# S4D convolution and PEER expert layer on one core: indices spread through DRAM, expert products on partitions, output as three rounded products

## The chip, the cores and the metric

The kernel runs on one core of a Trainium2 chip. The metric is the device time of one execution in microseconds. The core has five engines that run side by side, each in its own order: TensorE (PE in the rows, PEld for its weight loads), VectorE (DVE), ScalarE (ACT), GpSimd (POOL) and SyncE (SP), which here issues nearly all transfers.

## The reference

Sequence length 2048, width 512. Two stages with residuals; cut to what matters:

```
h  = x + S4D(layernorm(x))            # long convolution: kernel from 128 complex modes per channel, FFT of length 4096
xf = layernorm(h)
q  = einsum("nd,dhc->nhc", xf, w_q)   # 32 heads, two halves of 128
s1 = q[..., :128] . k1^T ; s2 = q[..., 128:] . k2^T     # 16 scores each
e  = 16*argmax(s1) + argmax(s2)       # one expert of 256 per token and head
act = gelu(einsum("nd,nhd->nh", xf, u[e]))
out = h + einsum("nh,nhd->nd", act, v[e])               # softmax over one candidate is 1
```

Since only one expert is chosen per head, the kernel needs per token only how often each of the 256 experts was chosen: `out = h + sum_e count[n,e] * gelu(xf[n]·u[e]) * v[e]`.

## The kernel before

**First part (to about 313 us).** The convolution as a two-step transform by matmuls, with tables of modes that POOL, ACT and DVE make (`factors`, `tables`, `kgen`, `u_s1` ... `k_ia`), and `w_piece`, which folds the keys into `w_q` and stores the product in DRAM (`w_d`).

**Second part (313 us to the end): the expert layer.** Eight blocks b of 256 tokens. Names end in the block's number, those of score work in 2b+k for its two halves of 128 tokens. For one block, in order of data:

- `prefetch`: `Tb`, `cb`, `xt` are loaded. `inverse`: 64 small matmuls (`ib`), DVE adds `xt`: `h`.
- `center`: POOL sums the four pieces of `h` (`hs`), a matmul with ones gives `mean`, DVE subtracts (`hc`), ACT rounds (`hhi`), DVE makes the rest (`hlo`), ACT squares `hc`. `variance`: POOL sums (`vs`), matmuls `var`, ACT root and DVE reciprocal give `rstd`, which is 128 tokens by 2.
- `scores`: for each half, four groups of six matmuls `sc`, as three rounded products (hi·hi, hi·lo, lo·hi) in float32r, and `xu`, tokens on partitions by 256 experts, in the same three products. DVE finds maxima (`mx`), marks them (`eq`), weighs them (`kq`), POOL sums (`ks`), DVE turns them into an index (`ei`, `ef`, `ix`). ACT takes `gelu(rstd*xu)` into `act`.
- `select`: PE transposes `act` (`ta`, ACT copies: `actT`) and `ix` (`ixt`, ACT copies: `ixT`, 32 heads by 256 tokens). Eight matmuls with a selection matrix (`bc`, line 1217) spread `ixT` so that partition 32j+i holds heads j; four ACT copies (line 1221) make `idxb`. DVE compares it with the expert codes, eight `oh` of 128x2048 (line 1239), matmuls `cnt` count, DVE multiplies with `actT` (`wt`), matmuls `o` (line 1269, plain float32) multiply with `v`, DVE adds `h` (`ob`), SP stores.

**What sets the order.** `Plan` records every step with an engine, a cost in us and its dependencies, then emits them greedily by list length (rank) plus a weight per group (`BIAS`). Each engine executes its instructions in that order. `REST` and `SLOW` are the plan's numbers for a slow PE clock after a rest. Buffers go round in rings (`RINGS`: three of `h`, two of `hhi`, `hlo`, `idxb`, one of `hc`, `ob`). PSUM holds two `sc` tiles (`psC`) and four others (`psD`). The last block works in two parts of 128 tokens:

```
    for b in range(8):
        prefetch(b)
        inverse(b)
        center(b)
        variance(b)
        scores(b, 0)
        scores(b, 1)
        select(b, ((0, 256),) if b < 7 else ((0, 128), (128, 128)))
    plan.EAGER = AHEAD
    plan.run(dict(PE=4.0, DVE=2.0, ACT=4.0, POOL=4.0, SP=4.2))
```

Of the kernel before, what the change touches and what calls it, by code (L numbers as in the profile page):

```python
# [27 lines left out]
def view(t, off, dims):  # L28
# [5 lines left out]
BIAS = dict(cen0=-321, cen1=200, cen2=494, cen3=497, cen4=149, cen5=340, cen6=-266, cen7=239, e1=358, ia0=-109,  # L34
            ia1=-262, ia2=137, ia3=-186, inv0=-5, inv1=276, inv2=455, inv3=28, inv4=-226, inv5=168, inv6=-279,
            inv7=251, k100=-188, k101=-367, k102=-393, k103=146, k110=-120, k111=-78, k112=285, k113=-195, k120=26,
            k121=138, k122=119, k123=500, k130=281, k131=65, k132=456, k133=-340, k20=1, k21=-267, k22=475, k23=455,
            par=1000, par0=-75, par1=482, pre0=-134, pre1=-400, pre2=-53, pre3=-248, pre4=22, pre5=-190, pre6=-358,
            pre7=-385, sc0=192, sc1=396, sc2=28, sc3=-3, sc4=-333, sc5=-351, sc6=208, sc7=-289, sel0=396, sel1=401,
            sel2=383, sel3=-57, sel4=143, sel5=-134, sel6=-243, sel7=-240, st=-225, tab0=-63, tab1=491, tab10=450,  # L40
            tab11=491, tab12=20, tab13=-259, tab14=96, tab15=242, tab16=320, tab17=48, tab18=-197, tab19=481,
            tab2=-105, tab20=-54, tab21=279, tab22=-344, tab23=-208, tab24=39, tab25=479, tab26=-241, tab27=-22,
            tab28=460, tab29=304, tab3=-332, tab30=-23, tab31=472, tab4=481, tab5=-171, tab6=6, tab7=-393, tab8=-37,
            tab9=-382, u100=-133, u101=99, u102=388, u103=473, u110=-377, u111=-173, u112=-171, u113=187, u120=-335,
            u121=439, u122=-81, u123=-23, u130=-213, u131=-7, u132=-347, u133=-341, u20=464, u21=-49, u22=164,
            u23=-320, var0=185, var1=-128, var2=-164, var3=178, var4=-12, var5=-16, var6=174, var7=157, w0=67,
            w1=-205, w2=320, w3=313, w4=-132, w5=344, w6=500, w7=54, wr=299)
# [3 lines left out]
class Plan:  # L51
# [5 lines left out]
    REST, SLOW = 3.0, 3.5  # L57
# [111 lines left out]
def kernel(ctx, tc, xa, xb, xt, lar, aim, cre, cim, ldt, dsk, wq, ka, kb, ue, ve,  # L169
# [16 lines left out]
    w_d = dram.tile([P, 4, 1024], F32, name="w_d")  # L186

# [270 lines left out]
    def stage1(dst, lhs8, kt, nm, r, tiles, key):  # L458
        for n in range(2):
            job = {}  # L460

            def mm(n=n, job=job):
                ps = bank(job, f"{nm}_{n}")
                for g in range(4):
                    for k in range(2):
                        T.matmul(ps[64 * k:64 * k + 64, g, :], lhs8(4 * n + g), c1_s[:, k], start=True, stop=True)  # L466

            def ev(n=n, job=job):
                A.copy(dst()[:, 8 * kt + 4 * n:8 * kt + 4 * n + 4].rearrange("p g k d -> p g (k d)"), job["ps"])  # L469

            k = plan.add("PE", 0.93, mm, r=r, t=tiles, take="psA", n_mm=16)
            plan.add("ACT", 0.48, ev, w=[key + (kt, n)], t=tiles, give="psA", after=[k])

    def stage2(c, nm, k4, deps, tiles):
# [10 lines left out]
        return job, plan.add("PE", 0.95, mm, r=deps + ["c2"], t=tiles, take="psA", n_mm=8)  # L485
# [183 lines left out]
    def kgen(i):  # L669
# [18 lines left out]
        plan.add("PE", 1.0, mm, r=[("tab", i, k, s) for k in range(2) for s in range(2)], w=[("kps", n)],  # L688
# [60 lines left out]
    def k_ia(c):  # L749
        plan.group = f"ia{c}"  # L750
        deps = [("P", c, k4) for k4 in range(8)]
        for n in range(8):
# [21 lines left out]
            k = plan.add("PE", 1.80, mm, r=deps + ["ca"], t=[f"yk{c}", f"yu{c}" if c > 2 else f"yk{c}", f"U{c}", f"T{c}"], take="psA", n_mm=16)  # L774
# [167 lines left out]
    def peer():  # L942
        wp = I["wp"]
        S["v"] = wp.tile([P, 2, D], F32, name="v_s")
        S["u"] = wp.tile([P, 4, 256], F32, name="u_raw")
# [5 lines left out]
    plan.add("SP", 0.9, peer, r=["hp"], w=["u", "v"], lag=6.0)  # L951
    plan.add("ACT", 0.95, lambda: A.copy(S["u_hi"], S["u"]), r=["u"], w=["u_hi"])
    plan.add("DVE", 1.15, lambda: V.tensor_sub(S["u_lo"], S["u"], S["u_hi"]), r=["u", "u_hi"], w=["u_lo"], lock=True)
    plan.add("DVE", 0.6, lambda: V.tensor_copy(S["sel"], S["sel_f"]), r=["sel_f", "hp"], w=["sel"], t=["sel_f"])
    L = [dict() for _ in range(8)]
    RINGS = dict(h=3, hs=2, vs=2, hc=1, hhi=2, hlo=2, rstd=2, act=2, mx=2, eq=2, kq=2, ks=2, ei=2, ef=2, ix=3,
                 actT=2, ixT=2, idxb=2, wt2=2, ob=1, Tb=2, cb=2, xt=2)
# [116 lines left out]
    def variance(b):  # L1074
# [4 lines left out]
        def mm():  # L1079
            ps = job["ps"] = I["psD"].tile([P, 2], F32, tag="m", name=f"var{b}")  # L1080
            for k in range(2):
                for q in range(4 if first else 1):
                    lhs = t["hc"][:, q] if first else t["vs"]
                    T.matmul(ps[:, k:k + 1], lhs[:, 128 * k:128 * k + 128], S["ones"][:, 0:1], start=(q == 0),
                             stop=(q == 3 or not first))

        def root():
            t["rstd"] = hp_("rstd", b, [P, 2])
            A.activation(t["rstd"], job["ps"], AF.Sqrt, bias=epst)

        kr = key("rstd", b)
        if first:
            k = plan.add("PE", 1.8, mm, r=["cst", kc], t=[kc, kr], take="psD", n_mm=16)
        else:
            kv = key("vs", b)
            plan.add("POOL", 2.4, sums(b, "vs", "hc", "vs"), r=[kc], w=[kv], t=[kc, kv])
            k = plan.add("PE", 0.45, mm, r=["cst", kv], t=[kv, kr], take="psD", n_mm=4)
        plan.add("ACT", 0.25, root, w=[kr], t=[kr], give="psD", after=[k], tab="sqrt")
        plan.add("DVE", 0.12, lambda: V.reciprocal(t["rstd"], t["rstd"]), w=[kr], t=[kr])

    def scores(b, k):
# [3 lines left out]
        job, jx, d = {}, {}, {}  # L1105
# [12 lines left out]
        def mx_():  # L1118
            ps = jx["ps"] = I["psD"].tile([P, 256], F32, tag="m", name="xu" + nm)
            for q in range(4):  # L1120
                for x_, w_ in terms:
                    T.matmul(ps, t[x_][:, q, ts], S["u_" + w_][:, q], start=(q == 0 and x_ == w_),
                             stop=(q == 3 and x_ == "lo"))

        ka_ = key("act", b) if k == 0 else f"act{b}"
        last = None
        for q in range(4):
            last = plan.add("PE", 1.45, lambda q=q: mm(q), t=tiles, after=[] if last is None else [last],
                            r=tiles + [("w_hi", q), ("w_lo", q)], take="psC" if q == 0 else None, n_mm=6)
        xk = plan.add("PE", 1.50, mx_, r=tiles + ["u_hi", "u_lo", f"rstd{b}"], t=tiles + [ka_, f"rstd{b}"], take="psD", n_mm=12)  # L1130
# [32 lines left out]
        def gelu():  # L1163
            act = tile_of(t, "act", lambda: hp_("act", b, [P, 2, 256]))
            A.activation(act[:, k], jx["ps"], AF.Gelu_apprx_tanh, scale=t["rstd"][:, k:k + 1])

# [5 lines left out]
        plan.add("ACT", 0.40, gelu, r=[f"rstd{b}"], w=[("act", b, k)], t=[ka_, f"rstd{b}"], give="psD", after=[xk],  # L1172
                 tab="gelu")

    def select(b, parts):
# [3 lines left out]
        kA, kB, kW, kO, kX = (key(a, b) for a in ("actT", "idxb", "wt2", "ob", "ixT"))  # L1179
        for k in range(2):  # L1180
            job = {}

            def mm(k=k, job=job):
                tp = job["ps"] = I["psD"].tile([P, 2, 128], F32, tag="m", name=f"ta{b}_{k}")
                for e in range(2):
                    T.transpose(tp[:, e, :], t["act"][:, k, 128 * e:128 * e + 128], ident)

            def ev(k=k, job=job):
                actT = tile_of(t, "actT", lambda: hp_("actT", b, [P, 2, 256]))
                A.copy(actT[:, :, 128 * k:128 * k + 128], job["ps"])  # L1190

            n = plan.add("PE", 0.22, mm, r=[("act", b, k)], t=[f"act{b}", kA], take="psD", n_mm=2)
            plan.add("ACT", 0.27, ev, w=[("actT", b, k)], t=[kA], give="psD", after=[n])
        for lo, ln in parts:
# [15 lines left out]
            hj = 512 // ln  # L1210
            for g in range(0, 8, hj):
                job = {}

                def mm(job=job, g=g, sl=sl, ln=ln, hj=hj):
                    job["ps"] = bp = I["psD"].tile([P, hj, ln], F32, tag="m", name=f"bc{b}_{g}_{ln}")
                    for h in range(hj):
                        T.matmul(bp[:, h], S["sel"][:, g + h, :], t["ixT"][:, sl], start=True, stop=True)

                def ev(job=job, g=g, sl=sl, hj=hj):
                    idxb = tile_of(t, "idxb", lambda: hp_("idxb", b, [P, 8, 256], BF16))  # L1220
                    A.copy(idxb[:, g:g + hj, sl], job["ps"])  # L1221

                n = plan.add("PE", 0.23, mm, r=[("ixT", p), "sel"], t=[kX, kB], take="psD", n_mm=hj)
                plan.add("ACT", 0.50, ev, w=[("idxb", p, g)], t=[kB], give="psD", after=[n])
            idx_k = [("idxb", p, g) for g in range(0, 8, hj)]
            job = {}
            cn = []
            for e in range(2):
# [23 lines left out]
                cn.append(plan.add("PE", 0.95 * ln / 256, mm, r=oh_k + ["cst"] + [("actT", b, k) for k in ks_], t=oh_k + [kW, kA], after=cn,  # L1252
                                   take="psD" if e == 0 else None, n_mm=32))

# [134 lines left out]
```

## Time and profile before

| | us |
|---|---|
| three runs | 537.65, 541.9, 542.56 (median 541.9) |
| profiled execution | 543.62 |
| its span, first to last instruction | 541.8 |
| PE busy | 466.3 (86% of the span) |
| DVE busy | 410.2 (76%) |
| POOL busy | 323.0 (60%) |
| ACT busy | 297.3 (55%) |
| mean granted PE clock | 0.974 |

Busy time is a mean over stages with different limits; matmuls overlap, so that a busy PE row is longer than the step from one start to the next. Where a price is wanted, the distance of starts in the timeline is taken.

### The profile page before, as it was taken

How to read it: one execution, taken by the hardware profiler on the slowest of the kernel's cores; microseconds unless marked ns; L12 is line 12 of the kernel's file. 1: busy time of each engine (PE TensorE's matmuls, PEld its weight loads, DVE VectorE, ACT ScalarE, POOL GpSimd, SP SyncE). 2: the span in 40 equal slices, each digit the busy share in tenths (PEclk: the TensorE clock that was granted, in tenths of full speed). 3: DMA queues.
4: the chain of work that ended last, by engine and by line, in shares of the span. 5: the costliest groups of instructions: out<-in, count | busy, mean ns of one | idle time of the engine just before them, and what ended most of it. 6: DMA issues, size and time to landing. Idle time of an engine off the chain costs nothing. (4 is left out here: it accounts for less than half of the span.)

```text
span 541.8 us, 16659 instructions
## 1 busy us (share of the span) xinstructions
PE 466.3 (86%) x7154; PEld 397.4 (73%) x7154; DVE 410.2 (76%) x716; ACT 297.3 (55%) x588; POOL 323.0 (60%) x339
## 2 busy tenths in 40 slices
PE   0045898989999999989995975999999999999996
PEld 0024677869999899979995964878777788888765
DVE  5997857779996898699738643368796695788884
ACT  6543888984899579949973612342323333406220
POOL 0698798999989999996817004161642535066030
PEclk9999799999999999999999888999999999999997
DMA  7984586667204120300065558000402511010011
GB/s 250 404 288 137 144 247 183 194 209 270 80 2 158 41 59 3 158 1 3 2 223 179 187 185 235 0 2 1 157 1 82 182 52 40 1 40 1 2 79 40
DMA packets 27361, 61.30 MB, mean 113 GB/s; under 512 B 2932, under 2 KB 14456, under 8 KB 26136
## 3 DMA queue, kind: packets, MB, share of 16 engines
q1 hardware_dynamic: 27136, 60.11, 33.3%
q8 instruction: 56, 0.92, 0.7%
q14 instruction: 17, 0.14, 0.1%
q10 hardware_dynamic: 152, 0.13, 0.1%
HBM read 46.21 MB, written 14.02 MB: 111 GB/s over the span
## 5 line engine op out<-in xcount | busy, mean ns | idle before, releaser
L552 POOL TENSOR_TENSOR pg<-PS 128x1024 int32<-128x1024 int32 x32 | 68.6, 2148 | 5.2 <-ACT t L639 5.1
L581 POOL TENSOR_TENSOR mg<-TS 128x1024 f32<-128x1024 f32 x32 | 62.6, 1956 | 13.8 <-PE kps L685 12.6
L1150 POOL TENSOR_TENSOR ks<-kq 128x512 f32<-128x512 bf16 x16 | 18.9, 1181 | 58.6 <-DVE kq L1144 58.6
L759 PE MATMUL ia<-ca_s,U 128*128 128x128 f32 x256 | 51.4, 284 | 0.7 <-POOL U L738 0.7
L1239 DVE TENSOR_SCALAR oh<-idxb,ec_s 128x2048 bf16<-128x2048 bf16 (+1 forms) x72 | 47.6, 729 | 5.2 <-ACT idxb L1221 5.2
L1115 PE MATMUL sc<-w_hi,hhi 128*128 128x512 f32 x128 | 45.5, 437 | 0.5 <-DVE eq L1139 0.5
L811 PE MATMUL wps<-wq,ka_s 128*32 128x128 f32 x256 | 15.4, 317 | 35.1 <-DMA wq<-wq 33.3
L640 ACT ACTIVATE t<-t,halfpi 128x512 f32<-128x512 f32 x64 | 42.4, 662 | 2.1
L759 PEld LDWEIGHTS ia<-ca_s,U 128*128 128x128 f32 x256 | 40.6, 200 | 1.0 <-POOL U L738 1.0
L639 ACT ACTIVATE t<-pg 128x512 f32<-128x512 int32 x64 | 39.4, 615 | 3.4 <-DVE gf L647 2.9
L1115 PE MATMUL sc<-w_lo,hhi 128*128 128x512 f32 x128 | 40.7, 400 | 0.0
L1115 PE MATMUL sc<-w_hi,hlo 128*128 128x512 f32 x128 | 40.6, 399 | 0.0
L642 ACT ACTIVATE t<-pg 128x512 f32<-128x512 int32 x64 | 39.2, 614 | 0.8 <-DVE U L730 0.3
L759 PE MATMUL ia<-ca_s,yk 128*128 128x128 f32 x192 | 38.2, 281 | 0.0
L466 PE MATMUL s1u<-c_s,xs 128*64 128x128 f32 x512 | 34.3, 279 | 4.1 <-DVE mg L659 1.1
L584 POOL TENSOR_TENSOR mg<-TS 128x512 f32<-128x512 f32 x32 | 37.4, 1169 | 0.0
L1029 POOL TENSOR_TENSOR hs<-h 128x256 f32<-128x256 f32 x7 | 7.3, 1038 | 48.8 <-DVE h L1012 48.8
L483 PE MATMUL s2yu<-yu,c_s 128*128 128x128 f32 x256 | 32.7, 282 | 4.2 <-DVE gf L647 1.7
L685 PE MATMUL kps<-mg 128*32 128x64 f32 x1024 | 34.1, 230 | 1.9 <-issue 1.0
L811 PEld LDWEIGHTS wps<-wq,ka_s 128*32 128x32 f32 x256 | 5.9, 117 | 40.1 <-DVE pa L329 31.4
L483 PEld LDWEIGHTS s2yu<-yu,c_s 128*128 128x128 f32 x256 | 30.0, 192 | 6.3 <-ACT yk L469 1.8
L466 PEld LDWEIGHTS s1u<-c_s,xs 128*64 128x64 f32 x512 | 28.3, 138 | 8.3 <-issue 4.3
(174 smaller groups left out, 1397.0 us busy)
## 6 DMA issues: line engine op xcount, KB each, us to landing
wq<-wq SPq DMA_DIRECT2D x32, 512.0 KB, 4.3
t_d<-T SPq DMA_DIRECT2D x24, 256.0 KB, 3.7
Tb<-t_d SPq DMA_DIRECT2D x8, 768.0 KB, 5.8
x<-xa SPq DMA_DIRECT2D x8, 512.0 KB, 6.2
xs<-xb SPq DMA_DIRECT2D x16, 256.0 KB, 6.2
xt<-xt SPq DMA_DIRECT2D x8, 512.0 KB, 5.7
out<-ob SPq DMA_DIRECT2D x7, 512.0 KB, 2.7
c_s<-c SPq DMA_DIRECT2D x1, 2048.0 KB, 14.3
```

Of the source, the lines that this page charges most:

```text
L466: T.matmul(ps[64 * k:64 * k + 64, g, :], lhs8(4 * n + g), c1_s[:, k], start=True, stop=True)
L483: T.matmul(ps[:, k, :], c2_s[:, kk, :], y[:, :, kk, :], start=True, stop=True)
L552: G.tensor_tensor(view(pg, 0, [[32, 2 * NC], [8, 4], [1, 8]]), view(t["PS"], 1024 + off, [[1, 2 * NC], [128, 4], [0, 8]]), view(t["PS"], 8 ...
L581: G.tensor_tensor(view(mg, 0, [[96, NC], [8, 8], [1, 8]]), view(ts, 512 + 8 * o, [[8, NC], [1, 8], [0, 8]]), view(ts, 8 * o, [[8, NC], [0, ...
L584: G.tensor_tensor(view(mg, 64, [[96, NC], [8, 4], [1, 8]]), view(ts, 1536 + o, [[1, NC], [64, 4], [0, 8]]), view(ts, 1024 + 8 * o, [[8, NC ...
L639: A.activation(p, pg[:, :, k], AF.Abs)
L640: A.activation(p, p, AF.Sin, scale=-SINSCALE, bias=halfpi)
L642: A.activation(p, pg[:, :, k], AF.Sin, scale=SINSCALE)
L685: T.matmul(kps[32 * q:32 * q + 32, 2 * g + h, :], m[:, d, 64:96], m[:, d, 0:64], start=(e == 0), stop=(e == 1))
L759: T.matmul(ps[:, g, :], t[:, 4 * n + g].rearrange("p a b -> p (a b)"), ca_s[:, s, :], start=(s == 0), stop=(s == 1))
L1115: T.matmul(ps[:, 512 * h:512 * h + 512], t[x_][:, q, ts], I[w_][:, q, 512 * h:512 * h + 512], start=(q == 0 and x_ == w_), stop=(q == 3 an ...
L1239: V.tensor_scalar(oh[:, :, 0:ln], t["idxb"][:, :, sl], S["ec"][:, 4 * e + j:4 * e + j + 1], None, op0=ALU.is_equal)
```

## The change

Four edits of the expert layer, and new numbers for the plan:

1. For blocks 0 to 6 `ixT` is stored to DRAM (`i_d`) and read back with each row repeated over 32 partitions, straight into `idxb`. `bc` and its ACT copies stay for block 7 alone.
2. `xu` is made with experts on partitions (`values`, after both halves of `scores`): the stationary operand is `u`, the moving one `hhi`/`hlo`. No transposes `ta` and no copies of them. `rstd` must then stand along the free dimension on all partitions: `var` is made with ones as the stationary operand (128x256), ACT's root and DVE's reciprocal run over 256 elements instead of 2, and DVE multiplies it in (`norm`), before a gelu over 512 elements.
3. `o` in three rounded float32r products. `v` is split into `v_hi`, `v_lo` once; per block ACT rounds the weights (`whi`), DVE makes the rest (`wlo`), each with one buffer.
4. `u` and `v` are loaded into buffers of the ring that `w_q` and `sel_f` used.
5. All of `BIAS`, `REST, SLOW = 2.6, 6.0`, and a few PE costs are new.

```diff
-            for k in range(2):
-                for q in range(4 if first else 1):
-                    lhs = t["hc"][:, q] if first else t["vs"]
-                    T.matmul(ps[:, k:k + 1], lhs[:, 128 * k:128 * k + 128], S["ones"][:, 0:1], ...
+                T.matmul(ps, S["ones"], t["vs"], start=True, stop=True)
...
-        plan.add("ACT", 0.25, root, w=[kr], t=[kr], give="psD", after=[k], tab="sqrt")
-        plan.add("DVE", 0.12, lambda: V.reciprocal(t["rstd"], t["rstd"]), w=[kr], t=[kr])
+        plan.add("ACT", 0.40, root, w=[kr], t=[kr], give="psD", after=[k], tab="sqrt")
+        plan.add("DVE", 0.35, lambda: V.reciprocal(t["rstd"], t["rstd"]), w=[kr], t=[kr], lock=True)
+
+    def values(b):
...
+                for u_, x_ in (("hi", "hi"), ("lo", "hi"), ("hi", "lo")):
+                    T.matmul(job["ps"][:, e], S["u_" + u_][:, q, 128 * e:128 * e + 128], t[x_][:, q],
+                             start=(q == 0 and u_ == x_), stop=(q == 3 and x_ == "lo"))
+
+        def norm():
+            t["actT"] = hp_("actT", b, [P, 2, 256])
+            V.tensor_tensor(t["actT"], job["ps"], t["rstd"].unsqueeze(1).to_broadcast([P, 2, 256]), op=ALU.mult)
...
+        n = plan.add("DVE", 0.62, norm, r=[kr], w=[kA], t=[kA, kr], give="psD", after=[last])
+        plan.add("ACT", 0.55, lambda: A.activation(t["actT"], t["actT"], AF.Gelu_apprx_tanh), ...
...
+            if b < 7:
+                def spread():
+                    t["idxb"] = hp_("idxb", b, [P, 8, 256], BF16)
+                    nc.sync.dma_start(t["idxb"], bass.AP(tensor=i_d.tensor, offset=i_d.offset + 8192 * b,
+                                                         ap=[[2048, 4], [0, 32], [1, 2048]]))
+
+                plan.add("SP", 0.5, lambda: nc.sync.dma_start(i_d[b].rearrange("j (g t) -> (j g) t", g=8), t["ixT"]),
+                         r=[("ixT", p)], w=[("i_d", b)], t=[kX], lag=2.5)
+                plan.add("SP", 0.6, spread, r=[("i_d", b)], w=[("idxb", p, 0)], t=[kB], lag=4.5)
...
+            n = plan.add("DVE", 0.62 * c_, mul, r=[kA], t=[kA], give="psD", after=cn)
+            n = plan.add("ACT", 0.52 * c_, high, r=[kA], w=[("whi", p)], t=[kA, kH], after=[n])
+            plan.add("DVE", 0.62 * c_, low, r=[kA, ("whi", p)], w=[("wlo", p)], t=[kA, kH, kL], lock=True, after=[n])
...
-                            T.matmul(ps[:, q], S["v"][:, e, 128 * (q0 + q):128 * (q0 + q) + 128], t["wt2"][:, e, sl],
-                                     start=(e == 0), stop=(e == 1))
+                            for v_, w_ in (("hi", "hi"), ("hi", "lo"), ("lo", "hi")):
+                                T.matmul(ps[:, q], S["v_" + v_][:, e, 128 * (q0 + q):128 * (q0 + q) + 128],
+                                         t["w" + w_][:, e, sl], start=(e == 0 and v_ == w_), stop=(e == 1 and v_ == "lo"))
```

The order of the first part is nearly the same in both, and both start `ib` of block 0 after the same PE work. Three places of the expert layer are shown.

DVE in front of block 1's comparisons (`oh8` to `oh15`). Before:

```order
L1139 TENSOR_TENSOR eq4_5192<-sc2_0_4943,mx4_5187 128x1024
L1144 TENSOR_TENSOR kq4_5209<-eq4_5192,key_s_4159 128x1024
L1051 TENSOR_TENSOR hc3_5221<-h3_5156,mean3_5211 128x1024
L1059 TENSOR_TENSOR hlo3_5250<-hc3_5221,hhi3_5234 128x1024
L1157 TENSOR_SCALAR ei4_5268<-ks4_5223 128x64
L1159 TENSOR_SCALAR ef4_5270<-ei4_5268 128x64
L1161 SCALAR_TENSOR_TENSOR ix4_5272<-ef4_5270 128x32
L1239 TENSOR_SCALAR oh8_5275<-idxb1_5248,ec_s_4160 128x2048
```

The same place after the change:

```order
L1165 TENSOR_TENSOR eq5_5114<-sc2_1_4902,mx5_5084 128x1024
L1302 TENSOR_TENSOR ob0_5123<-o0_0_0_5086,h0_4479 128x512
L1302 TENSOR_TENSOR ob0_5123<-o0_2_0_5101,h0_4479 128x512
L1170 TENSOR_TENSOR kq5_5157<-eq5_5114,key_s_4221 128x1024
L1183 TENSOR_SCALAR ei4_5176<-ks4_5116 128x64
L1185 TENSOR_SCALAR ef4_5178<-ei4_5176 128x64
L1187 SCALAR_TENSOR_TENSOR ix4_5180<-ef4_5178 128x32
L1021 TENSOR_TENSOR h3_5219<-ib3_0_5140,xt3_4570 128x4x128
L1021 TENSOR_TENSOR h3_5219<-ib3_1_5159,xt3_4570 128x4x128
L1257 TENSOR_SCALAR oh8_5240<-idxb1_5121,ec_s_4222 128x2048
```

Before, `hc3` and `hlo3` stood ahead of `oh8`, so that block 3's scores could follow on PE. Now block 0's output, both halves of block 2's scores and `h3` stand ahead of it, and `hc3`, `hlo3` come behind `oh15`. On PE the rows between the transposes `ixt1` and the first `cnt1` were four groups of `sc`, 24 `xu`, `mean3`, four `ta` and eight `bc`; now they are 24 `o0`, 24 `xu2` and 64 `ib3`, and no `sc`. PE's `o0` stands right behind `ixt1` and reads `wlo0`, which DVE makes after the last `cnt0`. In front of `cnt3`, likewise, PE now has `ixt3`, `o2`, `var4`, `ib5`, `ixt4`, `mean5` and no `sc`.

DVE around the reciprocal of block 4. Before, the reciprocal ran over 2 elements, with the scores behind it:

```order
L1059 TENSOR_TENSOR hlo5_5910<-hc5_5888,hhi5_5898 128x1024
L1239 TENSOR_SCALAR oh30_5945<-idxb3_5826,ec_s_4160 128x2048
L1239 TENSOR_SCALAR oh31_5954<-idxb3_5826,ec_s_4160 128x2048
L1099 RECIPROCAL rstd4_5886<-rstd4_5886 128x2
L1135 TENSOR_REDUCE mx8_5961<-sc4_0_5836 128x64
L1135 TENSOR_REDUCE mx9_5995<-sc4_1_5845 128x64
L1139 TENSOR_TENSOR eq8_6010<-sc4_0_5836,mx8_5961 128x1024
L1257 TENSOR_TENSOR wt23_6027<-cnt3_0_5912,actT3_5697 128x512
```

Now:

```order
L1257 TENSOR_SCALAR oh31_5947<-idxb3_5786,ec_s_4222 128x2048
L1060 TENSOR_TENSOR hc5_5949<-h5_5871,mean5_5900 128x1024
L1108 RECIPROCAL rstd4_5784<-rstd4_5784 128x256
L1276 TENSOR_TENSOR actT3_5671<-cnt3_0_5908,actT3_5671 128x512
L1068 TENSOR_TENSOR hlo5_6002<-hc5_5949,hhi5_5984 128x1024
L1282 TENSOR_TENSOR wlo3_6016<-actT3_5671,whi3_6000 128x512
L1257 TENSOR_SCALAR oh32_6019<-idxb4_5941,ec_s_4222 128x2048
```

`hc5` and the reciprocal now stand between the last comparison of block 3 and the multiplication (`actT3`, the former `wt`) that `o3` needs, and `wlo3` is new behind it.

SP's queue. Before, behind the loads for block 4:

```order
L979 DMA cb4_4656<-cb 128x512
L983 DMA xt4_4658<-xt 128x1024
L1278 DMA out<-ob0_5066 128x1024
L975 DMA Tb5_5164<-t_d_70 128x6x256
L979 DMA cb5_5167<-cb 128x512
L983 DMA xt5_5179<-xt 128x1024
```

Now:

```order
L988 DMA cb4_4660<-cb 128x512
L992 DMA xt4_4663<-xt 128x1024
L1223 DMA i_d_73<-ixT0_4869 32x256
L1220 DMA idxb0_4900<-i_d_73 128x1x2048
L1223 DMA i_d_73<-ixT1_5079 32x256
L1220 DMA idxb1_5121<-i_d_73 128x1x2048
L1306 DMA out<-ob0_5123 128x1024
L984 DMA Tb5_5233<-t_d_70 128x6x256
```

Each block's read waits in this queue for its own store to land, and the output of block 0 and the loads of block 5 stand behind block 1's pair.

More of the change, by code (lines that the diff above doesn't have):

```diff
@@ L1092, in variance @@
         if first:
-            k = plan.add("PE", 1.8, mm, r=["cst", kc], t=[kc, kr], take="psD", n_mm=16)
+            k = plan.add("PE", 1.75, mm, r=["cst", kc], t=[kc, kr], take="psD", n_mm=8)
         else:
@@ L1116, in mm @@
                              start=(q == 0 and x_ == w_), stop=(q == 3 and x_ == "lo"))
[L1118 to L1125, printed above, removed]
         last = None
         for q in range(4):
-            last = plan.add("PE", 1.45, lambda q=q: mm(q), t=tiles, after=[] if last is None else [last],
+            last = plan.add("PE", 1.48, lambda q=q: mm(q), t=tiles, after=[] if last is None else [last],
                             r=tiles + [("w_hi", q), ("w_lo", q)], take="psC" if q == 0 else None, n_mm=6)
-        xk = plan.add("PE", 1.50, mx_, r=tiles + ["u_hi", "u_lo", f"rstd{b}"], t=tiles + [ka_, f"rstd{b}"], take="psD", n_mm=12)
         m, e, kq_, s_, i_, f, x = (key(a, n) for a in ("mx", "eq", "kq", "ks", "ei", "ef", "ix"))
@@ L1178, in select @@
         t = L[b]
[L1179 to L1193, printed above, removed]
+        kB, kH, kL, kO, kX = (key(a, b) for a in ("idxb", "whi", "wlo", "ob", "ixT"))
+        kA = f"actT{b}"
         for lo, ln in parts:
@@ L1209, in select @@
             plan.add("ACT", 0.26, ev, w=[("ixT", p)], t=[kX], give="psD", after=[n])
[L1210 to L1224, printed above, removed]
```

126 lines of the change are left out of this document (82 added, 44 removed).

## The prediction

> **What bounds the kernel now.** I read the engines' shares by stage first, then PE's waits in the expert layer, then the chain that ends last, and last the single rows that price the edits. Two stretches (from:to, length, busy us of PE, weight loads, DVE, ACT, POOL, then granted clock, transfer share, GB/s):
>
> ```profile
> 333.10:533.40 200.30, 196.93 (x2085) 156.87 (x2084) 149.35 (x223) 65.10 (x108) 76.67 (x103) 0.98 0.15 51
> 385.00:410.00 25.00, 25.00 (x194) 18.95 (x196) 21.97 (x30) 9.04 (x15) 12.71 (x15) 1.00 0.21 69
> ```
>
> From 333.1 to 533.4 the expert layer runs, and PE is busy 196.9 of 200.3 us: it is idle for 3.4. DVE follows with 149.4, but unevenly: from 385 to 410 it has 22.0 of 25. ACT and POOL have room. PE's waits on others are tenths in that stretch (total us, times, longest), as for the two that the change bears on:
>
> ```profile
> PEld o L1269 <- DVE wt L1257: 0.6, 1, 0.6
> PE cnt L1249 <- DVE oh L1239: 0.2, 1, 0.2
> ```
>
> Only the end is not PE's. The chain that ended last (start, length) runs over the last block's comparisons on DVE, the count and `o`:
>
> ```profile
> 530.64 1.68 DVE oh L1239 x4
> ...
> 532.36 1.01 PE cnt L1249 x27
> 533.38 4.29 PE o L1269 x32
> ```
>
> So work taken from PE is worth its full length as long as PE stays fed, and work added to DVE costs where PE waits for DVE.
>
> **What PE loses.** PE's rows, each with the next row's start:
>
> ```profile
> 342.68 0.28 PE L1122 MATMUL xu<-u_hi,hhi 128*128 128x256 f32 x1
> 342.80 0.29 PE L1122 MATMUL xu<-u_lo,hhi 128*128 128x256 f32 x1
> ...
> 351.61 0.60 PE L1186 MATMUL ta<-ident,act 128*128 128x128 f32 x4
> 352.04 0.51 PE L1084 MATMUL var<-ones_d,vs 128*128 128x1 f32 x4
> ...
> 364.97 1.04 PE L1217 MATMUL bc<-ixT,sel_s 32*128 32x256 bf16 x8
> 365.94 0.74 PE L1115 MATMUL sc<-w_hi,hhi 128*128 128x512 f32 x2
> ...
> 373.69 1.06 PE L1249 MATMUL cnt<-oh,hs_s 128*32 128x256 bf16 x32
> 374.68 0.73 PE L1115 MATMUL sc<-w_hi,hhi 128*128 128x512 f32 x2
> 375.25 0.63 PE L1115 MATMUL sc<-w_lo,hhi 128*128 128x512 f32 x2
> 375.72 0.62 PE L1115 MATMUL sc<-w_hi,hlo 128*128 128x512 f32 x2
> 376.18 3.62 PE L1269 MATMUL o<-wt,v_s 128*128 128x256 f32 x16
> 379.45 0.82 PE L1115 MATMUL sc<-w_hi,hhi 128*128 128x512 f32 x2
> ...
> 381.12 0.26 PE L1005 MATMUL ib<-cb,Tb 128*32 128x64 f32 x3
> ...
> 383.04 0.74 PE L1115 MATMUL sc<-w_hi,hhi 128*128 128x512 f32 x2
> ...
> 527.61 5.76 PE L1249 MATMUL cnt<-oh,hs_s 128*32 128x128 bf16 x125 [0.18 <-DVE oh L1239]
> ```
>
> `bc` takes 0.97 us a block (365.94 - 364.97) and goes from seven: 6.8. `ta` takes 0.43, from eight: 3.4. `xu` keeps 24 matmuls of 256 columns at 0.12. `o` takes 3.27 for 16 instructions; 24 rounded ones at `xu`'s 0.12 take 2.88, so seven blocks save 2.7. Block 7's `o` has 128 columns, and no row has a rounded product that short: carrying on the step from 512 columns (0.23) to 256 (0.12) gives 0.06, 48 of them 3.0; at the pace of the plain `o` of 128 columns (4.29 / 32 = 0.134) they take 6.4. I take 3.0, since its kind of number is that of `xu`, a gain of 1.3, with a loss of 2.1 as the other end. `var` of block 0 shrinks by 0.2, the others stay at two instructions of `mean`'s kind for four short ones. Sum: 6.8 + 3.4 + 2.7 + 1.3 + 0.2 = 14.4 us less PE work.
>
> **What DVE gains.** Three instructions a block. `norm` and `wlo` go over 512 elements, as `wt` does. The reciprocal goes from 2 elements to 256; the first part shows its price by length.
>
> ```profile
> L328 DVE RECIPROCAL par<-par 128x112 f32<-128x112 f32 x4 | 3.5, 866 | 0.1
> L1099 DVE RECIPROCAL rstd<-rstd 128x2 f32<-128x2 f32 x8 | 1.2, 156 | 6.6 <-ACT rstd L1089 6.6
> L328 DVE RECIPROCAL par<-par 128x64 f32<-128x64 f32 x1 | 0.6, 566 | 0.0
> ...
> 402.39 0.68 DVE L1257 TENSOR_TENSOR wt<-cnt,actT 128x512 f32<-128x512 f32 x1
> 402.99 0.68 DVE L1144 TENSOR_TENSOR kq<-eq,key_s 128x1024 bf16<-128x1024 bf16 x1
> 403.59 1.22 DVE L1135 TENSOR_REDUCE mx<-sc 128x64 f32<-128x1024 f32 x1
> 404.84 1.23 DVE L1139 TENSOR_TENSOR eq<-sc,mx 128x1024 bf16<-128x1024 f32 x1
> ...
> 412.89 5.39 DVE L1239 TENSOR_SCALAR oh<-idxb,ec_s 128x2048 bf16<-128x2048 bf16 x8 [0.34 <-ACT idxb L1221]
> ```
>
> `wt` is 0.60 from start to start, so `norm` and `wlo` add 1.2. From 64 to 112 elements the reciprocal grows by 300 ns, 6.25 ns an element; 256 take 0.57 + 192 x 0.00625 = 1.77, against 0.16 now. The plan entered it with 0.35 (the diff), so the order was laid out for a DVE that is 1.4 us faster per block. In all 2.8 us a block, 22.6 in eight. If the slope came from PSUM operands alone, the nearest short row in SBUF (0.16) would be the lower end. [...] The row's 6.25 ns decides here.
>
> **What the index path gains.** Now: `bc` 0.97 and ACT copies, ended by the last of them. Then: a store of 16 KB, its landing, a read of 512 KB. No row has the read with rows repeated. Rows by size (KB each, us to landing):
>
> ```profile
> wq<-wq SPq DMA_DIRECT2D x32, 512.0 KB, 4.3
> xt<-xt SPq DMA_DIRECT2D x8, 512.0 KB, 5.7
> out<-ob SPq DMA_DIRECT2D x2, 256.0 KB, 2.3
> ka_s<-ka SPq DMA_DIRECT2D x1, 16.0 KB, 3.2
> ```
>
> Between 2.3 + 4.3 = 6.6 and 3.2 + 5.7 = 8.9; I take 7.5, with little else in the queue. ACT loses the copies, which PE had waited for only through `oh`.
>
> **Where it meets the new order.** Prices from the rows above: `sc` 1.41 a group of six (three pairs at 0.47), `ib` 1.8 to 1.9, `oh` 5.39 / 8 = 0.67, `mx` and `eq` 1.25 each, 0.6 for `wt`'s size; the index (three short instructions) and a cast on ACT I put at 0.6 too, an estimate.
>
> *Block 1.* Behind `ixt1` PE has only `o0` 2.9, `xu2` 2.9 and `ib3` 1.8 before `cnt1`: 7.6. `o0` waits 1.0 first for `wlo0` (multiply, cast, subtract after the last `cnt0`). DVE has from that `cnt0`, 1.4 before `ixt1`: multiply 0.6, `eq4` 1.25, `wlo0` 0.6, `mx5` 1.25, `kq4` 0.6, `eq5` 1.25, `ob0` 1.2, `kq5` 0.6, index 0.6, `h3` 1.3, four `oh` 2.7: 12.0, and about 0.1 at each of nine hand-overs: `cnt1` may start about 11.5 after `ixt1`, when PE has been free since 8.6: 2.9. The transfer (0.8 for the copy, then 7.5) is in by then, so DVE sets this. The other four `oh` take 2.7 against 1.0 of `cnt1`: 1.7. `o1` then waits for multiply, cast, `wlo1`: 2.1. Together 7.7.
>
> *Blocks 3 and 4.* After the last `sc4` PE has `ixt3`, `o2`, `var4`, `ib5`, 5.3 in all, then `ixt4`, which needs both indices of block 4: on DVE `mx`, `eq` twice, `kq`, `ob2`, `kq9`, `h5`, one `oh`, and POOL's sums: 10.5 from there. 5.2 idle; `mean5` 1.1 more (POOL's sum of `h5`), `cnt3` 0.5 and 1.7 for its two halves of `oh`, and `o3` 1.7, since `hc5` and the 1.77 of `rstd4` stand ahead of the multiplication: 10.2.
>
> *Blocks 4 to 7.* `sc6` needs `eq10`, late by `mean6` and `hc6`: 2.0. `ixt6` stands behind `ib7` alone, 3.3, `mean7` 1.0, `cnt5` 0.8 (`rstd6` ahead of its `oh`): 5.1. From about 510 to the end DVE sets the pace as it does now, with `rstd7`, `norm`, two `wlo` and the cast in it; PE stands 3.4 there.
>
> New waits: 7.7 + 10.2 + 2.0 + 5.1 + 3.4 = 28.4. They replace 5.2 of the old (3.4, and 1.8 in the last counts: 128 at the 0.031 of the row of 373.69 are 4.0, and took 5.8). Each change to another kind of matmul costs PE about 0.1 (374.68 to 375.25 is 0.57, a pair within a run 0.47); about 25 of them fall into these waits and cost nothing: -2.5. The first part has the same work, and I keep its time, plus or minus 3. The load of `u`, `v` now waits for buffers of the old ring; the first product that needs it, `xu0`, stands behind block 0's `sc`, so I cost it at nothing; a late one would show as a wait at `xu0`, once, of no more than the landing of 512 KB (4.3).
>
> Sum: -14.4 + 28.4 - 5.2 - 2.5 = +6.3 us on the profiled 541.8 us span, 548.1; with the 1.8 around it 549.9 against 543.62. That execution lies 1.7 above the median of the three runs, so on the median's scale 541.9 + 6.3, **548 us**. The main case's own range is 542 to 556: upwards 2.1 + 1.3 of `o`, 1.4 for the transfer at its slow end and 3 of the first part; downwards 3 of the first part and 3 of waits that end earlier.
>
> **Rivals.**
>
> *The gain stays (about 534).* If DVE gets through its list earlier than I add it up (a reciprocal at the short end takes 1.6 off every block, and its effect on `cnt5`, `o3` and the end with it), and the waits before `cnt1`, `ixt4` and `ixt6` come to 14 rather than 28.4, the sum is -14.4 + 14.0 - 5.2 - 2.5 = -8.1, about 534. For it: the 14.4 us of PE's work are gone for certain, while every wait is an addition of mine over ten and more rows. Against: the order shown has no `sc` between `ixt` and `cnt` in two blocks. With waits of 10 it is 530. It decides where `oh8` starts less than 9 us after `ixt1`.
>
> *DVE becomes the bound (about 556).* In the stretch 385 to 410 DVE has 22.0 of 25; with 2.8 more it is full. Where POOL's sums share its time, comparisons and index stretch: eight `oh` took 6.83 instead of 5.39 in
>
> ```profile
> 393.25 6.83 DVE L1239 TENSOR_SCALAR oh<-idxb,ec_s 128x2048 bf16<-128x2048 bf16 x8
> ```
>
> so a block takes 27 rather than 25, seven blocks +14. PE's rests add to it: after 5.0 us of rest a pair of `ia` took 0.43 (301.84 to 302.27), until 6.6 us later; from there 0.23:
>
> ```profile
> 295.22 0.61 PE L759 MATMUL ia<-ca_s,yu 128*128 128x128 f32 x2 [5.02 <-DVE yu L727]
> ...
> 301.84 0.60 PE L759 MATMUL ia<-ca_s,U 128*128 128x128 f32 x2
> 302.27 0.40 PE L759 MATMUL ia<-ca_s,yu 128*128 128x128 f32 x2
> 302.50 0.39 PE L759 MATMUL ia<-ca_s,U 128*128 128x128 f32 x2
> ```
>
> The rest before `ixt4` would cost 3.3 the same way if PE had work then. [...]
>
> *It comes out even (about 542).* The transfer and DVE's additions are hidden except at `ixt4` and the end: waits of 22, and the sum is -14.4 + 22 - 5.2 - 2.5 = -0.1.
>
> **How the numbers follow.** Main case 0.50, gain stays 0.26, DVE bound 0.18, even 0.06. About 1% (5.4 us) is what a measurement of this kernel can tell from no change. Of the main case's 542 to 556, 0.31 lies above 547.3 and 0.19 below; of the gain 0.25 lies under 536.5 and 0.01 above. Faster 0.25, same 0.19 + 0.06 + 0.01 = 0.26, slower 0.31 + 0.18 = 0.49. The range, 530 to 560, leaves out the gain's cases with waits under 10 and a third of the DVE-bound ones.
>
> **What would show it.** Right: reciprocals near 1.77 us; PE's busy time in the expert layer down by about 14 while its idle time there rises from 3.4 to over 20; PE waiting at `cnt` for `oh`, at `ixt` for `ix` and at `o` for `wlo`, longest before `ixt4`; the `idxb` read landing 4 to 6 us after its issue. Wrong: PE still idle for a few us only, or waits at `cnt` that a transfer ends and not DVE; a first part that is longer or shorter by more than 3; rounded `o` of 128 columns at plain pace.

## The result and the profile after

The changed kernel took 559.0 us (median; 556.1 to 560.3), the kernel before 542.1 beside it: a ratio of 1.032, interval 1.026 to 1.039. It is slower. Medians here are over all executions, but ratios and their intervals go by the faster ones of each kernel (within 1.5% of its fastest): the kernel before has both kinds, from 533 to 544 us. The profiled execution has a span of 557.7 us against 541.8, so 15.9 more.

I cut both spans at the first `ib`, where the expert layer begins. From:to, length, busy us of PE, weight loads, DVE, ACT, POOL, granted clock, transfer share, GB/s; first of the kernel before:

```profile
0.00:313.54 313.54, 254.84 (x4649) 227.86 (x4649) 250.05 (x479) 227.07 (x474) 242.43 (x233) 0.98 0.45 150
313.54:541.80 228.26, 211.42 (x2507) 169.58 (x2506) 160.16 (x238) 70.26 (x114) 80.54 (x106) 0.97 0.19 62
```

and of the kernel after:

```profile
0.00:309.64 309.64, 252.02 (x4648) 226.21 (x4649) 250.22 (x479) 226.89 (x474) 242.44 (x233) 0.99 0.45 151
309.64:557.70 248.06, 209.21 (x2469) 172.19 (x2468) 188.92 (x256) 56.25 (x72) 80.10 (x106) 0.90 0.23 74
```

The first part became 3.9 shorter, the expert layer 19.8 longer. In it PE's idle time went from 16.8 to 38.9 (length less busy): 22.0 more. The rise lies behind 333 us; up to there the two kernels rest alike, 9.3 and 8.3 us, at `ib` of block 1 above all. PE's busy time fell by 2.2 only, although by the forecast's count 14.4 us of matmuls are gone, and the granted clock stands at 0.90 instead of 0.97: the matmuls that are left got longer (the 448 `cnt` of 256 columns went from 274 to 311 ns).

PE's waits from 333 on, after (total us, times, longest):

```profile
PE ixt L1208 <- DVE ix L1187: 11.8, 4, 4.9
PE cnt L1267 <- DVE oh L1257: 5.7, 11, 3.4
PE bc L1235 <- ACT ixT L1212: 3.4, 2, 2.5
PE o L1297 <- DVE wlo L1282: 1.7, 3, 0.7
PE o L1297 <- ACT whi L1279: 1.3, 3, 0.8
```

Before, the longest wait of this kind was 0.6. The chain that ended last shows what stands behind `cnt` of block 1 (start, length):

```profile
376.13 1.39 DMA i_d<-ixT
...
377.54 9.61 DMA idxb<-i_d
...
387.18 5.73 DVE oh L1257 x8
...
392.95 1.53 PE cnt L1267 x26
```

The store takes 1.4, the read 9.6, and only then does DVE begin the eight comparisons; DVE had been idle for 1.9, and PE for 3.4 until the first of them was done:

```profile
387.18 5.72 DVE L1257 TENSOR_SCALAR oh<-idxb,ec_s 128x2048 bf16<-128x2048 bf16 x8 [1.87 <-DMA idxb<-i_d]
388.31 0.40 PE L1267 MATMUL cnt<-oh,hs_s 128*32 128x256 bf16 x1 [3.39 <-DVE oh L1257]
```

In front of `ixt4` it is the order on DVE, and the trip again through one row of that order. The index of the second half (`ei`, `ef`, `ix`, from 444.92) stands behind `h` of block 5 and the first comparison of block 3, which waits 2.6 for its own read, and PE rests 4.9:

```profile
440.38 1.28 DVE L1021 TENSOR_TENSOR h<-ib,xt 128x512 f32<-128x512 f32 x2
444.25 0.75 DVE L1257 TENSOR_SCALAR oh<-idxb,ec_s 128x2048 bf16<-128x2048 bf16 x1 [2.59 <-DMA idxb<-i_d]
444.92 0.21 DVE L1183 TENSOR_SCALAR ei<-ks 128x64 int32<-128x64 int32 x1
```

```profile
445.64 0.29 PE L1208 MATMUL ixt<-ident_b,ix 128*32 128x128 bf16 x1 [4.89 <-DVE ix L1187]
```

### The profile page after: what moved, and what is told of

It reads as the page before. It is cut to its first block, busy times and chain, and to the rows that moved or that the text cites. A ratio compares the mean times of both kernels' runs of the same rounds, so it can differ in the third digit from the quotient of the medians.

```text
span 557.7 us, 16562 instructions
## 1 busy us (share of the span) xinstructions
PE 461.2 (83%) x7116; PEld 398.4 (71%) x7116; DVE 439.1 (79%) x734; ACT 283.1 (51%) x546; POOL 322.5 (58%) x339
## 4 chain that ended last, share of the span: by engine, by line
PE 40%; DVE 26%; DMA 14%; ACT 13%; issue 4%; POOL 3%; SPq 0%; ACTq 0%; DVEq 0%; POOLq 0%
PE sc L1150 11%; PE ia L761 10%; DMA idxb<-i_d 9%; DVE oh L1257 4%; PE o L1297 3%; PE kps L687 3%; DVE U L732 3%; DVE yk L729 3%; DVE U L730 2%; ACT t L641 2%; ACT t L642 2%; ACT t L644 2%; PE s1k L468 2%; DMA i_d<-ixT 2%; DVE st L237 2%
## 5 line engine op out<-in xcount | busy, mean ns | idle before, releaser
L1150 PE MATMUL sc<-w_hi,hhi 128*128 128x512 f32 x128 | 43.8, 423 | 0.7 <-DVE eq L1165 0.7
L468 PE MATMUL s1u<-c_s,xs 128*64 128x128 f32 x512 | 32.8, 276 | 4.2 <-DVE U L732 1.4
L1038 POOL TENSOR_TENSOR vs<-hc 128x256 f32<-128x256 f32 x7 | 5.5, 784 | 52.3 <-ACT hc L1081 52.3
```

The source lines that it names most:

```text
L1150: T.matmul(ps[:, 512 * h:512 * h + 512], t[x_][:, q, ts], I[w_][:, q, 512 * h:512 * h + 512], start=(q == 0 and x_ == w_), stop=(q == 3 an ...
```

## The experiments

Three theories: the trip through DRAM is late (T); DVE's longer list is what PE waits for (D); the plan's entries or the new order are at fault (P, O). A fourth came up on the way: a rest costs twice, since PE's clock is low behind it (C; 0.50 was granted from 387.3 to 394.1, around the end of the rest before `cnt1` at 388.3).

### Four kernels that the plan orders anew, or not

**Edit 1 undone.** In `select`, so that `bc` and its copies serve all eight blocks:

```diff
-            if b < 7:
+            if False:
```

> The changed kernel with edit 1 undone: `bc` and its copies spread the indices in all eight blocks, nothing else differs, though the plan orders the rest anew. Theory T (the trip through DRAM is late: in the trace 1.4 us from the store to the read's issue and 8 to 10 us from there to the first `oh`, against about 3 for `bc` and copies): PE's rests at `cnt1` and in front of `ixt` go, +6.8 us of PE work comes back, and the time falls from 559 to about 545. Theory D (DVE's longer list, reciprocal, `norm`, `wlo`, is what PE waits for): `bc` is added on top, 559 to 566. Theory P (the plan's wrong entries set a bad order): 555 to 560, since the entry of the reciprocal is still wrong.

564.8 us, ratio 1.048 (1.039 to 1.057).

**Edit 1 alone**, in the kernel before, with its weights; the diff is the `if b < 7` branch of the change.

> The kernel before with edit 1 alone (trip through DRAM for blocks 0 to 6, the old weights). Theory T: PE waits for the late indices, gain of 6.8 us of `bc` more than eaten, 545 to 555. Theory D: the trip is hidden behind scores, 542 - 6.8 = 535 to 538.

571.9 us, 1.062 (1.052 to 1.072). Neither says much of the edit: taking a step out lets the plan lay out the whole list in another way, and while the first fits D, the second goes the way of T but lies far above the 545 to 555 that T gave. What they show is that the next trials have to hold the order fast.

**A short reciprocal.** It has the same plan entry, and in the trace every row of the expert layer keeps its place. It leaves out the reciprocal of 254 of the 256 elements, so that its output is not the layer's:

```diff
-... lambda: V.reciprocal(t["rstd"], t["rstd"]), ...
+... lambda: V.reciprocal(t["rstd"][:, 0:2], t["rstd"][:, 0:2]), ...
```

> The changed kernel in its own order, with the reciprocal over 2 of the 256 elements (the other 254 stay the root, so the weights are wrong there). It takes 1.6 us off DVE in each block. Theory D: the rests in front of `cnt`, `ixt` and `o` shrink, 8 to 12 us less, about 549. Theory T: DVE is not what comes last, 556 to 559; only the tail gives 1 to 2.

556.7 us, 1.031 (1.019 to 1.043). The reciprocal went from 1739 to 156 ns:

```profile
L1108 DVE RECIPROCAL rstd<-rstd 128x256 f32<-128x256 f32 x8 | 13.8, 1739 | 9.4 <-ACT rstd L1098 9.4
```

```profile
L1108 DVE RECIPROCAL rstd<-rstd 128x2 f32<-128x2 f32 x8 | 1.2, 156 | 7.1 <-ACT rstd L1098 7.1
```

DVE lost 12.6 us of work, and the time moved by 2.4, the ratio from 1.032 to 1.031, which isn't told from nothing. So the reciprocal, more than half of the 22.6 us that DVE was forecast to gain, is not the main cause, and D falls that far; `norm` and `wlo` were not taken out by themselves.

**The plan told the truth.**

```diff
-plan.add("DVE", 0.35, lambda: V.reciprocal(...
+plan.add("DVE", 1.75, lambda: V.reciprocal(...
-... w=[("i_d", b)], t=[kX], lag=2.5)
+... w=[("i_d", b)], t=[kX], lag=0.9)
-... w=[("idxb", p, 0)], t=[kB], lag=4.5)
+... w=[("idxb", p, 0)], t=[kB], lag=8.6)
```

(and 0.70 for `norm`, 0.75 for `wlo`.)

> The changed kernel with the durations of its trace entered into the plan (reciprocal 1.75 instead of 0.35, `norm` 0.70, `wlo` 0.75, the store's landing 1.4 instead of 3.0 from its issue, the read 9.2 instead of 5.1), which moves steps and changes no instruction. Theory P: 8 to 15 us less, 544 to 551. Theory T: the trip stays as long and the list has too little to put in its place, 553 to 560. Theory D: 555 to 560.

568.7 us, 1.056 (1.047 to 1.066): worse, outside all three. The true durations gave a worse list; that this is because the weights were fitted to the other durations is argued, not shown. P as I had put it is wrong; that the order itself may cost stayed open.

### The order held fast

For the next trials the plan's choice is replaced by a list of positions: a step goes out when its dependencies are out and its position is next.

```diff
-    plan.run(dict(PE=4.0, DVE=2.0, ACT=4.0, POOL=4.0, SP=4.2))
+    plan.pinned() if KEYS else plan.run(...)      # heap by KEYS[n], the step's place in the other kernel
```

The traces show how well the order is held. With the positions of the kernel after and edit 1 undone, the rows of the expert layer are those of the kernel after on every engine, with `bc` and its copies put in; in the last version below they are those of the kernel before, but for a few rows at the seam with the first part. So the edits and the order can be crossed. The edits are those of the diff, switched by `TRIP, XU, O3` (edits 1, 2 and 3); `O3` switches the buffers of edit 4 as well, so that this one is in no row by itself.

All three edits in the old order:

```diff
+TRIP, XU, O3 = (True, True, True)      # positions of the kernel before
```

> All three edits, but in the order of the kernel before: every step that both kernels have keeps its place on every engine; a new step stands at the place of the one that it replaces (store and read behind the copy `ixT`, `xu` in one piece at the place of the second half, `norm` and gelu behind it, `whi` and `wlo` behind the multiplication). Theory O (the new order is at fault, the edits are good): PE's work falls by 14, 530 to 540. Theory T (the trip is at fault in any order): the old order gives it even less time, 555 to 575. Theory D (DVE's added 2.8 us a block): 545 to 555.

None of them in the new order:

```diff
+TRIP, XU, O3 = (False, False, False)   # positions of the kernel after
```

> The order of the changed kernel with none of the edits: tokens on the partitions in `xu` and `ta`, `bc` in all blocks, plain `o`; each such step at the place of the one that had replaced it. This prices the order alone. Theory O: 560 to 575, slower than the changed kernel by the 14 us of PE work that comes back. Theory T: about 542 to 550, since what waits for the trip goes. Theory D: 545 to 552.

Edits 2 and 3 in the new order, so that against the kernel after edit 1 alone is undone:

```diff
+TRIP, XU, O3 = (False, True, True)     # positions of the kernel after
```

> The changed kernel in its own order, edit 1 alone undone: `bc` and its copies stand where the read stood, all other rows keep their place. Other than the first trial, nothing is ordered anew. Theory T: PE's rests shrink by more than the 6.8 us of `bc` that come back, 545 to 553. Theory O or D: the rests stay, 559 to 567.

Edit 1 in the old order:

```diff
+TRIP, XU, O3 = (True, False, False)    # positions of the kernel before
```

> The kernel before in its own order, edit 1 alone: the store and the read stand behind the copy `ixT`, `bc` and its copies leave, all else keeps its place. Theory T: `oh` comes about 7 us later per block (10.5 against 3), PE rests 3 to 5 of them, seven blocks: 555 to 575. Theory O: the 6.8 us of `bc` are gained, some of it lost in waits, 535 to 542; the 572 of the trial with the plan's new order would then be the order's.

Edit 2 in the new order:

```diff
+TRIP, XU, O3 = (False, True, False)    # positions of the kernel after
```

> The new order with edit 2 alone (experts on partitions in `xu`, the long reciprocal and `norm`; `bc` in all blocks, plain `o`). With none of the edits the order took 554.8, with edits 2 and 3 it took 561.4. If edit 2 costs (reciprocal and `norm` on DVE, 2.2 us a block): 560 to 563, and edit 3 is even. If edit 3 costs (two more hops to `o`, the rounded `o` of 128 columns in the last block, 8.3 us in place of 3.8): 551 to 555.

Edits 2 and 3 in the old order:

```diff
+TRIP, XU, O3 = (False, True, True)     # positions of the kernel before
```

> The old order with edits 2 and 3 and without the trip (`bc` stays). The old order takes 542 with none, about 581 with the trip alone and 591 with all. If the edits add up, 591 - 39 = 552. If the trip's lateness and DVE's additions hide in the same rests, more than that, 555 to 565. If edits 2 and 3 gain where nothing is late (7.6 us less PE work), 536 to 540.

Medians in us, ratio to the kernel before in the same session with its interval:

| edits | old order | new order |
|---|---|---|
| none | 542 (the kernel before) | 554.8, 1.025 (1.019 to 1.030) |
| 2 | | 553.1, 1.018 (1.010 to 1.025) |
| 2 and 3 | 552.3, 1.019 (1.013 to 1.024) | 561.4, 1.037 (1.031 to 1.043) |
| 1 | 581.5 (four executions: 569.2, the others 581.1 to 582.6) | |
| all | 591.0, 1.089 (1.082 to 1.097) | 559.0, 1.032 (1.026 to 1.039) |

Read by columns and rows: the new order alone costs 2.5% (12.5 us beside 542.3 in its session). In the profiles below, its expert layer is 15.2 us longer than that of the kernel before and its first part 4.5 shorter. In the new order, edits 2 and 3 cost another 6.6, and edit 1 then gives 2.4 or nothing (the intervals overlap). In the old order edit 1 costs 39 us on top of edits 2 and 3, and about as much by itself (27 to 40). So the new order is what edit 1 needs: it has taken some 40 us of the trip's lateness out of PE's way. But it pays 12.5 for that, and the trip has 6.8 us of `bc` to give. Edit 2 by itself isn't told from nothing in the new order (four executions, 548.2 to 559.2); most of the 6.6 is then edit 3's (with edit 4), by difference only. T holds in the old order, where the trip costs even more than its 555 to 575 with all edits, and fails in the new one. O is right that the new order costs, but wrong that the edits gain: in the old order they lose, and in the new one the kernel without them (554.8, put at 560 to 575) is no slower than the kernel with them. Neither theory alone stands.

The old order shows the trip's lateness bare. With edit 1 alone there, the waits of DVE and PE (in the execution of 581.8 us):

```profile
DVE oh L1353 <- DMA idxb<-i_d: 45.5, 7, 12.1
PE cnt L1363 <- DVE oh L1353: 26.8, 26, 5.7
```

DVE waits for the read in all seven blocks, 45.5 us in all. The expert layer (columns as in the windows above) in the new order with no edit, in the new order with edits 2 and 3, and in the old order with all:

```profile
309.07:552.50 243.43, 216.86 (x2507) 174.15 (x2506) 170.43 (x238) 69.61 (x114) 80.25 (x106) 0.94 0.17 59
309.82:558.40 248.58, 215.95 (x2525) 175.56 (x2524) 191.10 (x256) 70.64 (x100) 84.20 (x106) 0.92 0.18 59
310.85:590.90 280.05, 222.52 (x2469) 176.19 (x2468) 181.37 (x256) 56.40 (x72) 79.59 (x106) 0.87 0.21 66
```

The first of them has the same matmuls as the kernel before, yet PE is idle for 26.6 instead of 16.8 and busy for 216.9 instead of 211.4. The longest of its waits are again those in front of `ixt`, without any trip:

```profile
PE ixt L1303 <- DVE ix L1264: 7.1, 3, 3.9
```

From the second row to the kernel after, edit 1 takes 6.7 off PE's busy time (`bc`, by the forecast 6.8) and adds 6.2 of idle time (32.6 to 38.9). That is where its gain went. From the first row to the second, edits 2 and 3 remove 7.6 us of matmuls by the forecast's count, but busy falls by 0.9 and idle rises by 6.1.

### A rest filled

The kernel after, with products of the identity in front of the steps that wait longest, for instance

```diff
                 if e == 0:
                     job["ps"] = I["psD"].tile([P, 2, 256], F32, tag="m", name=f"cnt{b}_{lo}")
+                    if b == 1:
+                        warm(job["ps"][:, 0, 0:128], 26)
```

> The changed kernel with products of the identity put into PE's longest rests, written into the PSUM tile that the waiting step overwrites anyway: 3.6 us ahead of `ib1`, 3.0 ahead of `cnt1`, 2.0 and 4.5 ahead of the two halves of `ixt4`, 3.6 ahead of the second half of `ixt6`, 2.2 and 0.7 ahead of block 7's `bc`. No other row moves. Theory C (a rest costs twice: the wait and then PE's slower clock, 12 us of stretched matmuls in the expert layer): granted clock of that part from 0.90 towards 0.96, 5 to 9 us less, 550 to 554. If the stretch has another cause (memory traffic, weight loads), 558 to 562 with an unchanged clock.

582.4 us, 1.075 (1.070 to 1.080). The time is a miss of mine: a call made two instructions, and one of 64 columns took 0.113 us (17.63 for 156) like one of 128 (0.112: 52 of them from 381.0 to 386.7), so 58.8 us of products came instead of 19.6. From the windows, all of the expert layer (the same columns, PE to POOL), then those products alone:

```profile
308.11:579.40 271.29, 252.39 (x2981) 218.02 (x2980) 187.32 (x256) 56.24 (x72) 80.22 (x106) 0.99 0.21 68
```

```profile
308.11:579.40 271.29, 58.76 (x512) 0.99 0.21 68
```

What it was made for can be read all the same. The clock rose from 0.90 to 0.99, and the kernel's own matmuls, the same ones in the same order, took 252.4 - 58.8 = 193.6 us instead of 209.2 (194.6 when their own rows are joined, since neighbours overlap). So in the kernel after, some 15 us are the price of a lower clock. The kernel before, by the 14.4 us of matmuls that it was counted to have more, pays 211.4 - 193.6 - 14.4 = 3.4. C holds: the difference of 12.2 is what hid the gain in PE's work. The clock records of the traces give nearly the same without any count: in the expert layer PE was busy at half clock for 38.5 us in the kernel after, for 12.7 in the kernel before and for 5.7 with the rests filled; half of the differences is 16.4 and 12.9. Whether rests filled to their length bring the time down was not tried in this kernel.

### A version from the findings

None of the three edits: the expert layer in the old order, the first part in the new one, and 15 calls of such products in front of the first `ia` of the last quarter.

```diff
                 ps = bank(job, f"ia{c}_{n}")
+                if c == 3 and n == 0:
+                    warm(ps[:, 0, :], 15)
```

> A version from the findings, with none of the three edits: the expert layer in the old order, the first part's steps in the new order (its first `ib` started at 308.5 to 310.8 us in the kernels with the new order, at 310.9 to 314.9 in those with the old one), and 15 products of the identity ahead of the first `ia` of the last quarter, where PE rests for 4 to 5 us and then ran at half clock for 6.6. If both findings carry over: 3.5 less from the order and 2 to 3 from the clock, 535 to 537. If what follows the first part waits for transfers anyway (the rests ahead of `ib` take up the gain): 540 to 543.

535.0 us beside 542.1, ratio 0.994 (0.990 to 0.998): faster than the kernel before by half a per cent. The medians lie 7 us apart, but the kernel before ran from 533.8 to 544.2 in that session and this version from 534.3 to 536.8. The rest in front of `ia` is filled, and the clock from 288 to 303 stands at 1.00:

```profile
286.50 3.51 PE L794 MATMUL ia<-ident 128*128 128x128 f32 x30
290.61 0.49 PE L808 MATMUL ia<-ca_s,yu 128*128 128x128 f32 x2 [0.59 <-DVE yu L770]
...
309.59 0.33 PE L1068 MATMUL ib<-cb,Tb 128*32 128x64 f32 x3 [3.31 <-ACT T L821]
```

But PE then waits 3.3 at the first `ib` for ACT, and this `ib` starts at 309.6, no earlier than without the products (308.1 to 310.8 in seven of the eight kernels with the new weights, 313.9 in one): the faster `ia` only led to a wait elsewhere. So what the first part gained, 3.9 us, goes with its order, and the 535 to 537 that I had put down came out by luck: its 2 to 3 us from the clock are not there. The rest of the shorter span (533.0) lies in the expert layer, whose order is the old one; why its rests at `ib` are shorter in this profile is open:

```profile
309.50:533.00 223.50, 212.03 (x2506) 170.59 (x2506) 160.75 (x239) 69.54 (x112) 80.56 (x106) 0.96 0.19 65
```

## Why the prediction was right or wrong

The time came out at the upper edge of the range, 559.0 in 530 to 560; the forecast of "slower" held, the 6.3 us were 15.9 in the profile. The main case's own range ended at 556. The wide one holds 559.0 only because it reached over the rival of the bound DVE, which did not come true, and that is luck. Term by term, us:

| term | forecast | measured |
|---|---|---|
| PE's work | -14.4 | -17.8 (193.6 at a clock of 0.99 less 211.4 at 0.97) |
| waits, new less old | +23.2 | +22.0 |
| changes of the kind of matmul | -2.5 | in the other rows |
| matmuls at a lower clock | 0 | +15.6 |
| first part | 0 | -3.9 |
| sum | +6.3 | +15.9 |

- **PE's work and the waits** were right in the main. Of the work, `bc` could be priced by the difference of two kernels (6.7, forecast 6.8); the counted 14.4 leave 3.4 for the low clock of the kernel before. The waits came in their places too: block 1 with 3.4 and 1.1 at `cnt1`, 1.0 at `o0`, 1.5 at `o1`, together 7.0 (7.7 forecast); `ixt4` 2.5 and 4.9 and some tenths at `cnt3`, about 8 (10.2); `ixt6` 0.6 and 4.0 (with its neighbours 5.1); `sc6` 0.7 (2.0). In front of block 7's `bc` PE stood 3.4, a place that the forecast did not name.
- **The step that failed** is the clock. I had the price in hand, 3.3 us behind a rest of 5.0, but set it only into the rival of the bound DVE, and there once. The sum counted rests as if PE came out of them at full speed. It ran at half clock around and behind each long one, here those before `cnt1`, `ixt4` and `ixt6` (the 0.50 is the granted clock):

```profile
387.30:394.10 6.80, 4.55 (x59) 2.61 (x63) 6.71 (x12) 0.00 (x0) 0.41 (x1) 0.50 0.48 171
441.90:452.10 10.20, 5.87 (x68) 3.25 (x68) 7.78 (x13) 1.08 (x2) 2.01 (x3) 0.50 0.52 151
499.90:506.70 6.80, 5.31 (x23) 5.02 (x24) 6.73 (x9) 1.41 (x2) 1.08 (x2) 0.50 0.08 20
```

  The 12.2 us net are the whole gap between forecast and result, and more.
- **The transfer** was put at 7.5; store and read took 1.4 (once 3.0) and 7.8 to 9.9, where the forecast had the read land 4 to 6 after its issue. "DVE sets this" in block 1 was wrong: DVE idled 1.9 for the read, which is one of the forecast's own signs of being wrong. That the wait came out at its forecast size is partly luck.
- **The reciprocal** came at 1.74 (1.77 forecast). That it would matter was the rival's ground, and the short reciprocal shows 2.4 us by the medians, not told from nothing. So the rival "DVE becomes the bound" named nearly the right time, 556, for a reason that does not hold: from 333 to the end DVE is busy for 178 of 225 us.
- **`o` of block 7**: taken at 3.0, its other end 6.4; it took 8.3. At full clock a rounded product of 128 columns took 0.11 (545.60 to 547.61, 1.00 granted), at half 0.21 (from 547.7 on, 0.50), and the clock fell in it:

```profile
545.40:549.00 3.60, 3.56 (x26) 3.57 (x27) 0.81 (x2) 0.09 (x1) 0.00 (x0) 0.82 0.02 5
549.00:553.70 4.70, 4.70 (x23) 4.51 (x22) 0.31 (x1) 0.00 (x0) 0.00 (x0) 0.50 0.19 56
```

  The plain `o` took 3.78 for 32 in the new order without edits (0.118), and in the kernel before 0.11 each from 534.5 on, where 1.00 was granted: rounding saved nothing at this length, and there are three products for two. So even at full clock the 48 take about 5.3 (at 0.11): a loss of 1.0 to 1.5 stands where the sum had a gain of 1.3, and its 14.4 are some 2.3 too many. The forecast had named this plain pace as a sign of being wrong.

```profile
544.64 3.78 PE o L1401 x32
```

- **The first part** I kept; its steps are reordered on ACT, DVE and POOL as well, and its end came 3.9 earlier. A forecast sign of being wrong, a first part off by more than 3, is met as well. The last version keeps the new order there, and its first `ib` comes as early.
- **The gain stays** fails at its own point: it needed `oh8` less than 9 us after `ixt1` (375.3); it started at 387.2, 11.9 after it.

## What to carry to other kernels

Count a rest of the matmul engine at more than its length: here each us of idle time that a kernel had beyond the kernel before came with 0.45 to 0.8 us of stretched matmuls in ten of eleven kernels, and 1.2 in the other, edits 2 and 3 in the old order (busy time less the matmuls as the forecast counted them, over idle time, from first `ib` to the end). A change of steps and the order fitted to it must be priced apart: hold the order fast by the old kernel's positions, cross the two, and a gain on paper of 14 us shows as 12.5 lost to the order, and edits that bring no gain even in it (559.0 against 554.8, with intervals that overlap). And before replacing on-chip work by a round trip, time the trip as the chain sees it: store, landing, read, here about 10 us for what `bc` and copies did in 3.

## What the runs showed of the hardware

The read with repeated rows was twice as slow as a plain load of the same 512 KB (7.8 to 9.9 us against a median of 4.2 for `wq`). While it ran with little else, the transfer engines were busy for a sixth, at 65 GB/s, which is 512 KB in 8.1 us:

```profile
358.80:366.90 8.10, 8.10 (x46) 7.00 (x46) 6.64 (x9) 1.76 (x2) 5.49 (x8) 1.00 0.17 65
449.50:457.40 7.90, 7.45 (x74) 6.34 (x72) 5.80 (x8) 4.01 (x4) 1.41 (x2) 0.83 0.18 66
```

So it is no queueing: by itself the read kept few of the 16 engines busy (0.17 of their time). The packet records of the trace bear this out: the read at 358.8 is 128 packets of 4 KB with 0.16 us each (median), of which four were under way together for 4.5 of the 6.1 us and never more than six; of the plain loads from 40 to 45 us in the kernel before, packets of the same size, 16 and more ran together at the height. The source of the read starts with a dimension of 4, and four packets went at a time; that the one sets the other is not shown. A source whose outermost dimension is the 32 repetitions, with the expert codes permuted to suit, was not tried. If its read took the plain load's 4.2 instead of 8.1, it would take some 4 us off each trip, an estimate from these two times.

In the kernel after, the lower clock cost about 15 of 557.7 us (209.2 less 193.6), over 2.5%, since the rests come again in block after block: the clock records have eight stretches at 0.50 in its expert layer, and four in that of the kernel before.
